# Two tiles of a chunked attention prepared a block earlier, and the second expert's rows turned on TensorE

## The chip, the cores and the metric

The kernel runs on one core of a Trainium2 chip. The metric is the device time of one execution in microseconds (us); below, "the median" is that of three runs. One further execution was profiled.

## The reference

Three layers follow each other: a gated linear attention, a gated two-matrix layer, and a layer of eight experts of which each token uses one.

```python
f = 1.0 / (1.0 + np.exp(-f_logit))                  # q, k, v, f_logit: 4 x 8 x 768 x 48
for t in range(S):                                  # per batch and head, state 48 x 48
    state = f[:, :, t, :, None] * state + np.einsum('bhd,bhe->bhde', k[:, :, t], v[:, :, t])
    y[:, :, t] = np.einsum('bhd,bhde->bhe', q[:, :, t], state)
x = y.transpose(0, 2, 1, 3).reshape(3072, 384)      # tokens x model
x = ((x @ w_a) * (x @ w_b)) @ w_out                 # 384 x 1536, 384 x 1536, 1536 x 384
logits = x @ w_gate; e_idx = argmax(logits, axis=1) # 8 experts
...
for e in range(8):                                  # w1: 384 x 1024, w2: 1024 x 384
    mask = e_idx == e
    ye = np.maximum(x[mask] @ w1[e], 0.0) @ w2[e]
    out[mask] = gate_w[mask, None] * eom[mask, e, None] * ye
```

## The kernel before, in words

Products in full precision are made of three passes on TensorE over a number split into a high and a low part (`xh`, `xl`; `wab` and `wo` hold both parts of the weights). Everything is unrolled; the program is one long list for each engine.

**Attention tiles.** The 768 positions of 4 batches are 24 tiles of 128 positions, `order[i] = (c, b)`: chunk by chunk, batch by batch. A tile goes through the steps of the list `steps` (L1038): `a_log` (step 0: sigmoid's logarithm on ScalarE, its halves `lh` and `ll`), `a_v` (1), `a_range` (2: sums of squares for a range test, and the loads of tile i+2), `a_cum` (3: a running sum on TensorE, L791 and L792, and two exponentials `eq`, `ek`), `a_q` (4), `a_z` and `a_vs` (5: the halves of q and k laid side by side in `z` by VectorE and GpSimd, then a DMA transpose of `z` into `zT` issued by SP at L835), `a_u` and `a_uh` (6: the state's decay and halves), `a_kv` (7), `a_score` (8: L919, L926 on TensorE, then `sm`, `Sh`, `Sl`), `a_av` (10), `a_turn` (12) and `a_x` (13: the tile turned, as `xh` and `xl`). Inputs and most tiles have two buffers.

**Blocks.** Two tiles make a block of 256 tokens, `j` from 0 to 11; a block needs 12 steps `f` of `m_ab` (L1063 to L1065), each followed by `asb` (ScalarE), `gf` (VectorE), `gh` (ScalarE), `gl` (GpSimd) and `m_out` (L1098 to L1100). `r_row`, `r_pick`, `r_rank` and `r_send` then choose each token's expert and scatter its place into `slots`.

**First phase.** The conversion of the weights, tiles 0 to 5 and blocks 0 and 1 are generators in the list `threads`, each with a start time. `in_time` (L508) runs a small model of the engines over them, picks in its order and chains each engine's instructions in that order. In the profile this phase ends at about 164 us.

**Later blocks.** For `j` from 2 to 11, step `f` runs `m_ab`, `m_out`, the routing of block j-1 and `attend(2j+2, f)`, which runs those steps of tiles 2j+2 to 2j+5 whose entry in the table `at` (L1262) is this `f`. So tiles 6 and 7 pass from step 1 (tile 7: from step 1 as well) to `a_x` while TensorE works on block 2, and tile 8 starts in its last step. Outside the first phase the framework orders each engine's list itself, by a simulation at build time in which program order is the priority; an instruction marked with `keep_in_program_order` (or `in_order`) stays behind all that was written before it on its engine. On the chip every engine then works through its list in order.

**Experts.** The first place (the fullest expert, e = 0) has 512 slots, worked on in two halves of 256, each with 8 steps `f`: `e_h` (L1465 to L1467: product, `h` by a Relu on ScalarE at L1479, the low part by VectorE at L1483) and, one step behind, `e_y` (the matmuls of L302 into `ps_out` and `ps_yk`). The rows come by gathers on GpSimd (`xs`, L1363); those of the first place are turned by TensorE in `to_columns` (L1453, then L1454 and L1455). The second place's rows (e = 1, four tiles, 480 slots) are turned as 16-bit halves: a copy on VectorE and a DMA transpose issued by SP in `e_turn` (L1425, L1430), and two copies on VectorE, one on ScalarE and a subtraction in `e_xT` (L1441 to L1446). Expert weights come in 8 pieces of 384 KB into `raw` (three buffers); `load_epiece` issues a load on SP and `split_expert` makes the halves on ScalarE (L1244) and VectorE (L1245), both kept in program order. Three pieces of the second place are loaded in the first place's first half and split in its steps 4 to 6; the other five are loaded and split in steps 0 to 4 of its second half:

```python
            if f == 2:
                e_gather(1)
                load_epiece(1, split=False)
            if f >= 4 and fetched:
                split_expert()
...
        elif half == 1:
            ahead(1, TURN1, XT1, f)
            load_epiece(1)
```

Of the kernel before, what the change touches and what calls it, by code (L numbers as in the profile page):

```python
# [305 lines left out]
def kernel(  # L306
# [413 lines left out]
    def a_log(i):  # L720
        yield op("ACT", 0.5, ("in_f", i))
        s = st[i]
        f = s["f"]
        nc.scalar.activation(out=f, in_=f, func=AF.Exp, scale=-1.0)
        yield op("ACT", 0.7, gives=("ln", i))
        nc.scalar.activation(out=f, in_=f, func=AF.Ln, scale=c_st, bias=c_st)
        yield op("DVE", 0.4, ("ln", i), ("cum", i - 1), gives=("lh", i))
        s["lh"] = tl("lh", [P, H, D], F16)
        nc.vector.tensor_copy(out=s["lh"], in_=f)
        yield op("DVE" if i < NFAST else "POOL", 0.6 if i < NFAST else 1.0, ("lh", i), gives=("ll", i))  # L730
        s["ll"] = tl("ll", [P, H, D], F16)
        fast(i).tensor_tensor(out=s["ll"], in0=f, in1=s["lh"], op=ALU.subtract)
# [85 lines left out]
    def a_z(i):  # L818
        yield op("DVE", 0.37, ("kx", i), ("T", i - 2), ("kv", i - 2), gives=("kh", i))
        s = st[i]  # L820
        z = s["z"] = z_n[i % NZ]
        qe, ek = [s[x].rearrange("p (a o) d -> p a o d", o=2) for x in ("qe", "ek")]
        kh, kl = z[:, :, 6:10:3, :D], z[:, :, 7:9, :D]
        nc.vector.tensor_copy(out=kh, in_=ek)
        yield op("DVE" if i < NFAST else "POOL", 0.58 if i < NFAST else 1.0, ("kh", i), gives=("kl", i))
        fast(i).tensor_tensor(out=kl, in0=ek, in1=kh, op=ALU.subtract)
        for o in range(2):
            yield op("DVE", 0.37, ("qe", i))
            q2 = qe[:, :, o, None, :].to_broadcast([P, HP, 2, D])
            nc.vector.tensor_copy(out=z[:, :, 2 * o : 2 * o + 2, :D], in_=q2)  # L830
        yield op("DVE", 0.58, gives=("ql", i))
        nc.vector.tensor_tensor(out=z[:, :, 4:6, :D], in0=qe, in1=z[:, :, 0:4:2, :D], op=ALU.subtract)
        yield op("SP", 3.1, ("ql", i), ("kl", i), ("scored", i - 2), *inter_of(i - 2), gives=("T", i), lands=0.6)
        s["T"] = tl("zT", [P, 5 * HP, P], F16, 2)
        nc.sync.dma_start_transpose(out=s["T"], in_=z.rearrange("p a c d -> p (a c d)"))  # L835

    def a_vs(i):
        yield op("DVE", 0.42, ("vv", i), ("kv", i - 1), gives=("vs", i))
        s = st[i]
        s["vs"] = tl("vs", [P, 2, H, D], F16)  # L840
        nc.vector.tensor_scalar(out=s["vs"], in0=s["vv"], scalar1=c_w, scalar2=None, op0=ALU.mult)

    def a_u(i):

        c, b = order[i]
        if c < NCH - 1:
            for o in range(2):
                yield op("SP", 0.45, ("gd", i), ("U", i - 2), gives=("g", i, o), lands=0.05)
                s = st[i]
                g = s["g"] = g_n[i % 2]  # L850
                nc.sync.dma_start(g[part(o)], s["gd"][:].rearrange("(a o) d -> d a o", o=2)[:, :, o])

    def a_uh(i):
        c, b = order[i]
        if c > 0:
            for o in range(2):
                yield op("ACT", 0.37, ("U", i - 2), *inter_of(i - 2), gives=("uh", i, o))
                s = st[i]
                u2, u3 = s["u2"], s["u3"] = U2[i % 2], U3[i % 2]
                hi, lo = u2[part(o), :, o], u2[part(1 - o), :, o]  # L860
                nc.scalar.activation(out=hi, in_=U[b][part(o)], func=AF.Copy)
                yield op("POOL", 0.6, ("uh", i, o))
                nc.gpsimd.tensor_tensor(out=lo, in0=U[b][part(o)], in1=hi, op=ALU.subtract)
                yield op("POOL", 0.4, gives=("u", i, o))
                nc.gpsimd.tensor_copy(out=u3[part(o), :, o], in_=hi)
# [146 lines left out]
    def a_x(i):  # L1012
# [23 lines left out]
        nc.vector.tensor_tensor(out=xl[:, :, ts], in0=x, in1=xh[:, :, ts].bitcast(F32), op=ALU.subtract)  # L1036

    steps = [  # L1038
        a_log, a_v, a_range, a_cum, a_q, lambda i: both(a_z(i), a_vs(i)), lambda i: both(a_u(i), a_uh(i)), a_kv,
        a_score, None, a_av, None, a_turn, a_x,  # L1040
    ]

    def both(x, y):
        yield from x
        yield from y
# [193 lines left out]
    def split_expert():  # L1239

        e, g, part, raw, tag, nk = fetched.pop(0)
        pair = ring_tile(tag)
        hi, lo = pair[:, :768], pair[:, 768:1536]
        in_order(tc, nc.scalar.activation)(out=hi, in_=raw, func=AF.Copy)  # L1244
        nc.vector.tensor_tensor(out=lo, in0=raw, in1=hi.bitcast(F32), op=ALU.subtract)  # L1245
        we[e, g, part] = (
            hi.rearrange("p (k f) -> p k f", k=nk),
            lo.rearrange("p (k f) -> p k f", k=nk),
        )
# [3 lines left out]
    def load_epiece(e, split=True):  # L1253
        if e < E and epieces[e]:
            load_expert(*epieces[e].pop(0))
            if split:
                split_expert()
# [8 lines left out]
    def route(j, f):  # L1266
# [5 lines left out]
        if f == 3:  # L1272
            r_rank(j)
            r_send(j)

    def attend(i0, f):

        for i, g in ((i0, f), (i0 + 2, f - NF)):
            for t in range(2):
                if i + t < NTILE:  # L1280
                    for n in range(14):
                        if at[t][n] == g and steps[n]:
                            run(steps[n](i + t) or ())

# [28 lines left out]
    for i in range(6):  # L1313
        for t, gen in (
            (0, a_log(i)), (3, a_v(i)), (2, a_cum(i)), (3, a_q(i)), (4, a_z(i)), (6, a_vs(i)), (4, a_u(i)), (4, a_uh(i)),
            (8, a_kv(i)), (9, a_score(i)), (12, a_av(i)), (14, a_x(i)),
        ):
            threads.append((T0[i] + t, gen))
    for n in range(len(batches)):
        t = C0 + CD * n  # L1320
        threads.append((t - 6, raw_load(n)))
        threads.append((t, (conv_o if batches[n][0] == "o" else conv_ab)(n)))
        if batches[n][0] == "o":
            threads.append((t - 9.4, gates(n)))
# [33 lines left out]
    def tiles_of(e):  # L1358

        return [(t, min(P, CAPS[e] - t)) for t in range(0, CAPS[e], P)]  # L1360
# [108 lines left out]
    def e_h(e, f, n=None):  # L1469

        us = slice(0, CAPS[e]) if e > 0 else slice(n * HALF, (n + 1) * HALF)
        size = us.stop - us.start
        ph = bank("ab")[:, :size]
        first_product(e, f, ph, us)

        h = ctl("h", [P, 2 * CAP], F32R, 4)
        t, m = tiles_of(e)[-1]
        cut = t if e > 0 and is_pair(m) else 0
        nc.scalar.activation(out=h[:, :size], in_=ph, func=AF.Relu)  # L1479
        for lo, hi in ((cut, size), (0, cut)):  # L1480
            if hi > lo:
                to = size + lo - cut if lo >= cut else 2 * size - cut + lo
                nc.vector.scalar_tensor_tensor(  # L1483
                    out=h[:, to : to + hi - lo],
                    in0=ph[:, lo:hi],
                    scalar=0.0,
                    in1=h[:, lo:hi].bitcast(F32),
                    op0=ALU.max,
                    op1=ALU.subtract,
                )  # L1490
        h_t[e, f, n] = (h, size, cut)
# [139 lines left out]
        nc.vector.tensor_reduce(out=bad, in_=tot, axis=AX, op=ALU.max)  # L1631
        nc.vector.tensor_copy(out=flag, in_=bad)

    TURN1, XT1 = [0, 0, 2, 2], [4, 5, 6, 7]
    TURN, XT = [2, 2, 3, 3], [4, 5, 6, 7]

    def ahead(e, turn, columns, f):

        for u in range(NU):
            if turn[u] == f:  # L1640
                e_turn(e, u)
            if columns[u] == f:
                e_xT(e, u)
# [50 lines left out]
    for n in range(1, 2 * NF2 + LAG):  # L1694
        half, f = divmod(n, NF2)
        if half < 2:
            e_h(0, f, half)
        if n >= LAG:
            done, fy = divmod(n - LAG, NF2)
            for u in range(2):  # L1700
                e_y(0, fy, 2 * done + u)
                if fy == NF2 - 1 and done == 0:
                    e_out(0, u)
        if half == 0:
            if f == 2:
                e_gather(1)
                load_epiece(1, split=False)
            if f >= 4 and fetched:
                split_expert()
            if f == 6:  # L1710
                for e in range(2, E):
                    find(e)
                    load_tab(e)
            if f == 7:
                for u in range(2):
                    to_columns(0, xs[0][:, 2 + u], slice((2 + u) * P, (3 + u) * P), idn)
        elif half == 1:
            ahead(1, TURN1, XT1, f)
            load_epiece(1)
    for e in range(1, E):  # L1720
        for f in range(NF2):
            e_h(e, f)
# [65 lines left out]
```

## Time and profile before

| what | value |
|---|---|
| median of 3 runs | 886.93 us (883.01 to 887.08) |
| the profiled execution, its own time | 891.19 us |
| its span, first to last instruction | 889.1 us |
| mean granted TensorE clock over the span | 0.973 of full speed |
| TensorE busy | 814.3 us, 92% of the span, 6733 matmuls |
| VectorE, ScalarE, GpSimd busy | 542.2, 450.7 and 300.3 us |

The profile is of one execution, and 4.3 us longer than the median; 2.1 us of it lie outside the span. Busy shares are means over stages that have different limits; places where TensorE stands idle are found by windows, and what it waits for by the waits and the timeline.

### The profile page before, as it was taken

How to read it: one execution, taken by the hardware profiler on the slowest of the kernel's cores; microseconds unless marked ns; L12 is line 12 of the kernel's file. 1: busy time of each engine (PE TensorE's matmuls, PEld its weight loads, DVE VectorE, ACT ScalarE, POOL GpSimd, SP SyncE). 2: the span in 40 equal slices, each digit the busy share in tenths (PEclk: the TensorE clock that was granted, in tenths of full speed). 3: DMA queues.
4: the chain of work that ended last, by engine and by line, in shares of the span. 5: the costliest groups of instructions: out<-in, count | busy, mean ns of one | idle time of the engine just before them, and what ended most of it. 6: DMA issues, size and time to landing. Idle time of an engine off the chain costs nothing.

```text
span 889.1 us, 17901 instructions
## 1 busy us (share of the span) xinstructions
PE 814.3 (92%) x6733; PEld 773.5 (87%) x6733; DVE 542.2 (61%) x1244; ACT 450.7 (51%) x1068; POOL 300.3 (34%) x383
## 2 busy tenths in 40 slices
PE   2599899969999999999999999999779999999993
PEld 1398799969999999999999899999779889899993
DVE  8899763636765656566666556436446665666730
ACT  5798765345655546555555453335224433544520
POOL 3013442535445444444444353220442123111111
PEclk9999799989999999999999999999889999999997
DMA  9997683481836262626270803005375585585610
GB/s 212 298 265 177 118 175 57 68 83 28 141 51 118 47 122 46 123 46 123 44 125 20 149 19 78 20 19 160 116 202 131 146 198 115 156 195 150 183 45 23
DMA packets 261578, 102.06 MB, mean 115 GB/s; under 512 B 229032, under 2 KB 252933, under 8 KB 261482
## 3 DMA queue, kind: packets, MB, share of 16 engines
q1 hardware_dynamic: 256362, 90.76, 47.6%
q0 software_dynamic: 4320, 10.03, 4.2%
q8 instruction: 55, 0.90, 0.5%
q14 instruction: 41, 0.34, 0.2%
q10 hardware_dynamic: 800, 0.02, 0.1%
HBM read 67.10 MB, written 10.49 MB: 87 GB/s over the span
## 4 chain that ended last, share of the span: by engine, by line
PE 61%; DMA 13%; issue 8%; DVE 8%; ACT 4%; SPq 3%; POOL 1%; another core or an unknown queue 1%; POOLq 0%; DVEq 0%; ACTq 0%
PE ps_ab L1063 10%; PE ps_ab L1064 9%; PE ps_ab L1065 9%; PE ps_out L1098 5%; PE ps_out L1099 5%; PE ps_out L1100 5%; DMA turned<-halves 4%; DMA in_f<-in_f_logit_dram 3%; PE ps_out L302 2%; PE ps_yk L302 2%; DMA raw<-in_moe_w_dram 2%; PE ps_ab L1465 2%; PE ps_ab L1466 2%; PE ps_ab L1467 2%; PE ps_yk L973 1%
## 5 line engine op out<-in xcount | busy, mean ns | idle before, releaser
L1063 PE MATMUL ps_ab<-xh,wab 128*128 128x256 f32 x864 | 247.9, 287 | 4.4 <-DVE gf L1071 3.5
L1064 PE MATMUL ps_ab<-xl,wab 128*128 128x256 f32 x864 | 244.1, 283 | 0.2
L1065 PE MATMUL ps_ab<-xh,wab 128*128 128x256 f32 x864 | 243.6, 282 | 0.0
L1080 POOL TENSOR_TENSOR gl<-gf,gh 128x256 fp32r<-128x256 f32 x135 | 105.8, 785 | 220.6 <-ACT gh L1077 214.9
L1063 PEld LDWEIGHTS ps_ab<-xh,wab 128*128 128x128 f32 x864 | 163.5, 189 | 9.8 <-DVE gf L1071 6.8
L1064 PEld LDWEIGHTS ps_ab<-xl,wab 128*128 128x128 f32 x864 | 163.5, 189 | 1.5 <-DVE xl L1036 0.9
L1065 PEld LDWEIGHTS ps_ab<-xh,wab 128*128 128x128 f32 x864 | 163.5, 189 | 0.8
L1071 DVE SCALAR_TENSOR_TENSOR gf<-ps_ab,asb 128x256 f32<-128x256 f32 x144 | 60.2, 419 | 76.7 <-ACT asb L1068 73.7
L1098 PE MATMUL ps_out<-wo,gh 128*128 128x400 f32 x288 | 103.3, 359 | 2.9 <-ACT ex L1146 2.5
L1099 PE MATMUL ps_out<-wo,gh 128*128 128x400 f32 x288 | 100.5, 349 | 0.0
L1077 ACT ACTIVATE gh<-gf 128x256 fp32r<-128x256 f32 x144 | 59.9, 416 | 79.4 <-DVE gf L1071 76.4
L1100 PE MATMUL ps_out<-wo,gl 128*128 128x400 f32 x288 | 98.5, 351 | 0.0
L1068 ACT ACTIVATE asb<-ps_ab 128x256 f32<-128x256 f32 x144 | 54.4, 378 | 68.1 <-PE ps_ab L1065 67.7
L1539 POOL DMA_INDIRECT out_dram<-ys,tab x29 | 30.0, 1033 | 166.7 <-ACT ys L1534 160.3
L1465 PE MATMUL ps_ab<-xsh,wab 128*128 128x256 f32 (+5 forms) x216 | 74.1, 344 | 4.5 <-DVE h L1483 4.5
L1466 PE MATMUL ps_ab<-xsl,wab 128*128 128x256 f32 (+5 forms) x216 | 73.7, 341 | 0.1
L1467 PE MATMUL ps_ab<-xsh,wab 128*128 128x256 f32 (+5 forms) x216 | 73.5, 340 | 0.0
L1479 ACT ACTIVATE h<-ps_ab 128x256 fp32r<-128x256 f32 (+5 forms) x72 | 34.7, 483 | 76.1 <-PE ps_ab L1467 51.2
L1483 DVE SCALAR_TENSOR_TENSOR h<-ps_ab,h 128x64 fp32r<-128x64 f32 (+5 forms) x96 | 41.2, 451 | 39.8 <-ACT h L1479 39.5
L1245 DVE TENSOR_TENSOR wab<-raw,wab 128x768 fp32r<-128x768 f32 x48 | 45.8, 956 | 31.9 <-ACT wab L302 26.9
L1098 PEld LDWEIGHTS ps_out<-wo,gh 128*128 128x128 f32 x288 | 55.0, 191 | 4.1 <-ACT ex L1146 3.1
L302 ACT ACTIVATE wab<-raw 128x768 fp32r<-128x768 f32 x48 | 40.3, 841 | 31.5 <-DMA raw<-in_moe_w_dram 31.1
(241 smaller groups left out, 1700.8 us busy)
## 6 DMA issues: line engine op xcount, KB each, us to landing
raw<-in_moe_w_dram SPq DMA_DIRECT2D x64, 384.0 KB
in_f<-in_f_logit_dram SPq DMA_DIRECT2D x24, 192.0 KB
in_q<-in_q_dram SPq DMA_DIRECT2D x24, 192.0 KB
in_k<-in_k_dram SPq DMA_DIRECT2D x24, 192.0 KB
in_v<-in_v_dram SPq DMA_DIRECT2D x24, 192.0 KB
wab<-in_moe_w_a_dram SPq DMA_DIRECT2D x6, 768.0 KB
wab<-in_moe_w_b_dram SPq DMA_DIRECT2D x6, 768.0 KB
wo<-in_moe_w_out_dram SPq DMA_DIRECT2D x6, 768.0 KB
```

The costliest lines, as they stand in the source:

```text
L302: return lambda *a, **k: tc.keep_in_program_order(op(*a, **k))
L1063: nc.tensor.matmul(pab[:, a], wh[:, kk, o : o + P], xh[:, kk], start=(kk == 0), stop=False)
L1064: nc.tensor.matmul(pab[:, a], wh[:, kk, o : o + P], xl[:, kk], start=False, stop=False)
L1065: nc.tensor.matmul(pab[:, a], wl[:, kk, o : o + P], xh[:, kk], start=False, stop=(kk == KD - 1))
L1071: nc.vector.scalar_tensor_tensor(out=gf, in0=pab[:, 1], scalar=2.0**-WS, in1=asb, op0=ALU.mult, op1=ALU.mult)
L1080: (nc.vector if last else nc.gpsimd).tensor_tensor(out=gl, in0=gf, in1=gh.bitcast(F32), op=ALU.subtract)
L1098: nc.tensor.matmul(o, gh[:, ts], wh[:, u], start=(f == 0), stop=False)
L1099: nc.tensor.matmul(o, gh[:, ts], wl[:, u], start=False, stop=False)
L1100: nc.tensor.matmul(o, gl[:, ts], wh[:, u], start=False, stop=(f == NF - 1))
L1465: nc.tensor.matmul(ph, wh[:, kk, o : o + P], sh[:, kk, us], start=(kk == 0), stop=False)
L1466: nc.tensor.matmul(ph, wh[:, kk, o : o + P], sl[:, kk, us], start=False, stop=False)
L1467: nc.tensor.matmul(ph, wl[:, kk, o : o + P], sh[:, kk, us], start=False, stop=(kk == KD - 1))
```

## The change

Two parts of the program are rearranged.

First, `a_log`, `a_v`, `a_cum`, `a_q`, `a_z`, `a_u` and `a_uh` of tiles 6 and 7 become threads of the first phase, with start times 110 and 118; `attend` leaves out these steps (the tuple `begun`) for tiles below 8, and step 5 runs `a_vs` alone for them. `a_range`, `a_vs`, `a_score` and what follows stay where they were.

Second, for the first place (e = 0) every Relu of `e_h` is kept in program order on ScalarE. No piece of the second place's weights is split in the first half any more: each step of the second half issues one load (as long as there are pieces) and makes one split, so the eight splits fall on its eight steps. The second place's rows are turned by `to_columns` on TensorE in steps 4 to 7 of the second half, one tile a step; its `e_turn` and `e_xT` go away. Experts 2 to 7 are as before.

```diff
     steps = [
-        a_log, a_v, a_range, a_cum, a_q, lambda i: both(a_z(i), a_vs(i)), lambda i: both(a_u(i), a_uh(i)), a_kv,
+        a_log, a_v, a_range, a_cum, a_q, lambda i: a_vs(i) if i < NPE + 2 else both(a_z(i), a_vs(i)), lambda i: both(a_u(i), a_uh(i)), a_kv,
         a_score, None, a_av, None, a_turn, a_x,
     ]
...
+    begun = (0, 1, 3, 4, 6)
+
     def attend(i0, f):
 
         for i, g in ((i0, f), (i0 + 2, f - NF)):
             for t in range(2):
                 if i + t < NTILE:
                     for n in range(14):
+                        if i + t < NPE + 2 and n in begun:
+                            continue
                         if at[t][n] == g and steps[n]:
                             run(steps[n](i + t) or ())
...
+    for i in range(NPE, NPE + 2):
+        for gen in (a_log(i), a_v(i), a_cum(i), a_q(i), a_z(i), a_u(i), a_uh(i)):
+            threads.append((110 + 8 * (i - NPE), gen))
...
-        nc.scalar.activation(out=h[:, :size], in_=ph, func=AF.Relu)
+        ins = nc.scalar.activation(out=h[:, :size], in_=ph, func=AF.Relu)
+        if e == 0:
+            tc.keep_in_program_order(ins)
...
-    TURN1, XT1 = [0, 0, 2, 2], [4, 5, 6, 7]
...
             if f == 2:
                 e_gather(1)
                 load_epiece(1, split=False)
-            if f >= 4 and fetched:
-                split_expert()
...
         elif half == 1:
-            ahead(1, TURN1, XT1, f)
-            load_epiece(1)
+            if f == 0:
+                xsT[1] = (ctl("xsh", [P, KD, CAP], F32R, 2), ctl("xsl", [P, KD, CAP], F32R, 2))
+            if f >= 4:
+                t, m = tiles_of(1)[f - 4]
+                to_columns(1, xs[1][:m, f - 4], slice(t, t + m), idn[:m, :m])
+            load_epiece(1, split=False)
+            split_expert()
```

## Rows read from the trace of the kernel before

**Rows 1.** Windows of core 0: time, busy time of each engine, granted clock, DMA share, GB/s.
```profile
119.00:164.00 45.00, 45.00 (x427) 43.62 (x426) 17.43 (x41) 25.62 (x74) 13.39 (x21) 1.00 0.44 86
164.00:204.00 40.00, 31.98 (x321) 29.86 (x321) 24.61 (x61) 18.05 (x51) 18.84 (x22) 0.91 0.79 88
204.00:564.00 360.00, 356.69 (x3494) 341.51 (x3493) 227.76 (x559) 190.47 (x513) 164.32 (x218) 1.00 0.44 78
...
634.00:645.00 11.00, 6.14 (x27) 5.54 (x27) 4.44 (x7) 4.24 (x8) 7.46 (x7) 0.69 0.68 198
645.00:671.00 26.00, 20.97 (x124) 20.03 (x123) 13.88 (x30) 8.95 (x19) 10.28 (x10) 0.87 0.66 179
```

**Rows 2.** Timeline of TensorE, 176 to 200 us; in brackets the wait before.
```profile
179.92 0.40 PE L919 MATMUL ps_at<-zT 128*128 128x128 f16 x4 [1.40 <-DMA zT<-z]
...
186.43 0.59 PE L919 MATMUL ps_at<-zT 128*128 128x128 f16 x4 [4.99 <-DVE dj L1193]
...
189.07 0.41 PE L1063 MATMUL ps_ab<-xh,wab 128*128 128x256 f32 x1
...
189.70 0.28 PE L1063 MATMUL ps_ab<-xh,wab 128*128 128x256 f32 x1
```

**Rows 3.** Timelines of SP, ScalarE and VectorE, 164 to 202 us.
```profile
169.94 3.02 SPq L835 DMA_TRANSPOSE zT<-z  x1
173.02 0.57 SPq L302 DMA_DIRECT2D in_f<-in_f_logit_dram  x1
...
177.94 9.38 SPq L835 DMA_TRANSPOSE zT<-z  x1
...
184.56 0.52 ACT L724 ACTIVATE in_f<-in_f 128x384 f32<-128x384 f32 x1 [5.98 <-DMA in_f<-in_f_logit_dram]
...
185.86 0.36 DVE L729 CAST lh<-in_f 128x384 f16<-128x384 f32 x1 [7.73 <-ACT in_f L726]
```

**Rows 4.** Timeline of TensorE, 630 to 702 us.
```profile
637.18 1.01 PE L302 MATMUL ps_out<-wab,h 128*128 128x384 f32 x2 [3.23 <-ACT wab L302]
639.87 0.90 PE L1453 MATMUL ps_at<-idn,xs 128*128 128x128 f32 x3 [1.69 <-DMA xs<-x2d,tab]
...
644.07 0.49 PE L1453 MATMUL ps_at<-idn,xs 128*128 128x128 f32 x3
...
645.14 0.51 PE L1465 MATMUL ps_ab<-xsh,wab 128*128 128x256 f32 x2
...
658.47 2.29 PE L302 MATMUL ps_yk<-wab,h 128*128 128x384 f32 x6 [4.80 <-ACT h L1479]
...
668.52 0.28 PE L1465 MATMUL ps_ab<-xsh,wab 128*128 128x256 f32 x1
...
670.64 0.37 PE L1465 MATMUL ps_ab<-xsh,wab 128*128 128x480 f32 x1
```

**Rows 5.** Timelines of ScalarE, SP and GpSimd, 612 to 700 us.
```profile
636.01 0.84 ACT L302 ACTIVATE wab<-raw 128x768 fp32r<-128x768 f32 x1 [5.82 <-DMA raw<-in_moe_w_dram]
...
658.04 0.38 ACT L1479 ACTIVATE h<-ps_ab 128x256 fp32r<-128x256 f32 x1 [6.90 <-remote]
...
632.83 1.02 SPq L302 DMA_DIRECT2D raw<-in_moe_w_dram  x2
...
636.05 1.01 POOL L1363 DMA_INDIRECT xs<-x2d,tab  x1 [0.31 <-issue]
```

**Rows 6.** Waits: ScalarE 204 to 600 us, TensorE 200 to 600 and 60 to 160.
```profile
ACT in_f L724 <- DMA in_f<-in_f_logit_dram: 26.8, 9, 4.7
...
PE ps_out L1098 <- ACT ex L1146: 1.8, 1, 1.8
...
PE ps_at L791 <- POOL ll L732: 0.7, 1, 0.7
```

**Rows 7.** The chain that ended last, 620 to 700 us: start, length, what.
```profile
634.70 4.76 DMA xs<-x2d,tab
...
687.26 6.79 DMA raw<-in_moe_w_dram
```

## What the change was predicted to do

> **What bounds the kernel now.** I read the windows first. TensorE is busy 814.3 of 889.1 us by the page, and in the long middle it is the bound without a doubt: 3.3 us idle in 360 us, about 0.4 in 40 us [rows 1]. So a change can win only where TensorE is not fed, and I looked for those places. Two lie where this change works. Place A, 164 to 204 us, is block 2: 8.0 us idle. Place B, 634 to 671 us, is the middle and second half of the first expert's place: 4.9 and 5.0 us idle. In both the granted clock is under 1, so part of the work ran at 1.2 instead of 2.4 GHz [rows 1]. The other idle stretches (the start, and the last expert's end) are not touched.
>
> Then the timelines, to see what TensorE waited for. In A it is 1.4 us for the DMA transpose of tile 6 and 5.0 us for VectorE [rows 2]. VectorE was late because a cast for tile 8 (L729) stood in its list behind the logarithm of ScalarE, which waited 5.98 us for the load of `in_f` [rows 3]. That load was issued at 173.02, right behind the transpose of tile 6 that held SP for 3.02 us, and landed at 184.5, 11.5 us later; the transpose of tile 7 then held SP for another 9.38 us [rows 3]. So the reader is to see that an input load for the next tiles, late among two transposes, stops two engines that work through fixed lists. After it the products ran at 1.2 GHz (one 0.41 us long) up to 189.7, where they are 0.28 us again [rows 2].
>
> In B the first stop is ScalarE standing 5.82 us in the split of a weight piece while finished products wait for their Relu behind it; TensorE loses 3.23 us, and then waits 1.69 us more for the gathered rows of the second half [rows 4, 5]. The second stop is 4.80 us before 658.47. The Relu that ends it began at 658.04 after 6.90 us of idleness for which the profile names no releaser ("remote") [rows 4, 5]; I know only that the second expert's four DMA transposes, which the change removes, run there.
>
> **The change part by part, place A.** Running sum, exponentials, `z`, its transpose and the state's halves of tiles 6 and 7 move into block 1, 119 to 164 us. Is there room? TensorE is full there (45.00 of 45), but VectorE has 27.6, ScalarE 19.4 and GpSimd 31.6 us free. All that these three did in 164 to 204 (24.6, 18.1, 18.8), block 2's own work included, would fit, and the moved part is less than that [rows 1]. SP's two transposes go past the stores and loads of block 1, at 3 us each as the first one shows [rows 3]. So I cost the moved work at nothing on these engines. If that cover failed, the wait would fall on TensorE, whose fixed list holds the two running sums in between products. The nearest row is a running sum of an earlier tile that waited 0.7 us for its operand [rows 6]: 0 to 1.4 us for two; I take 0.7.
>
> What is won: 8.0 us idle, and the 3.3 us from 186.43 to 189.70 at the lower clock, which cost 1.6: 9.6 us. What is late next is tiles 8 and 9, whose loads and logarithms keep their places; they no longer queue behind two transposes. In the middle stretch ScalarE still waits nine times for `in_f`, 26.8 us together, and TensorE hardly notices [rows 1, 6]. The rest of idleness is then between 0.4 us (a mean 40 us of the middle) and everything but the 1.4 us wait for the transpose. I leave 2.0, near the middle's end, since the jam of SP is what differs from the middle. A: 9.6 - 2.0 - 0.7 = 6.9 us; ends 9.2 and 0.
>
> Here the trace speaks against a rule. A transpose held SP 3.02 and 9.38 us where the load of `in_f` took 0.57, and TensorE saw tile 6's transpose landed at 179.92, 10.0 us after its issue [rows 2, 3]. The Trainium skill, "Advanced Engine Details and Errata", section "X-Bar Transpose (TRN2)", says that "TRN2 transpose DMAs are as fast as regular DMAs". By that rule moving them frees little, the late load stays late, and the third rival below is what happens; by the rows the sum stands.
>
> **Place B.** The three splits leave the first half, so no Relu stands behind a load there. From 633.95 (where the 3.23 us wait begins) TensorE has left two products of first-half steps and what follows them, two pairs; a pair takes 2.12 us (668.52 to 670.64) [rows 4]: done at 638.2. Then it must wait for the gather: the first landed at 639.46, the second was issued at 636.05, and with the same 4.76 us lands at 640.8 [rows 5, 7]. From the transposes to the next product took 1.07 us (644.07 to 645.14) [rows 4]; with 0.4 for the start, as between 639.46 and 639.87, the second half starts at 642.3 instead of 645.14.
>
> From there to the second expert's first product it took 25.5 us (645.14 to 670.64). The work in it now is 7.5 pairs, 15.9 us, since the first half's last `e_y` is already done, and the new cost, four tiles turned on TensorE at 0.49 us each [rows 4], 2.0 us. The second expert starts at 642.3 + 17.9 = 660.2, which is 10.4 us earlier. The copies taken off VectorE and the four transposes off SP are not on the path and count as nothing. From this I take off three things.
>
> The clock: after the long wait the work from 639.87 to 645.14 ran under a window mean of 0.69, 5.3 us at 1.2 GHz at the most, which costs 2.6 [rows 1, 4]; the wait that is left is shorter, so 0 to 2.6, and I take 1.3.
>
> The weights: pieces 4 to 8 each need one of three buffers, which comes free only after a split in this half. One turn of a buffer is the load, 0.4 us of issue, 0.84 of cast [rows 5] and about 1 for the subtraction; a load took 3.2 us (632.83 to 636.01) at best and 6.8 at worst [rows 5, 7]. At 3.2 a turn is 5.4 us, at 6.8 it is 9.0, against three steps of 2.12, 6.4 us. Two turns: 0 to 5.3 us late. Behind a late split stand the next Relu on ScalarE and so TensorE. I take 1.5, as the stretch has fewer transfers than the one with 6.8.
>
> The Relu's fixed place behind the routing's exponentials and row copies at about 623 us: 0 to 1 us, I take 0.3, since other products are ready.
>
> B: 10.4 - 1.3 - 1.5 - 0.3 = 7.3 us; ends 10.4 and 1.5. [...]
>
> **Sum.** 6.9 + 7.3 = 14.2 us: the profiled execution would go from 891.2 to 877.0. It lies 4.3 us above the median of the runs, so I take 14.2 off 886.9: 872.7 us.
>
> **The rivals.** (1) The weight loop sets the pace: loads at 6.8 us take all 5.3. B is 10.4 - 1.3 - 5.3 - 0.3 = 3.5, the total 876.5. For it: one turn at 3.2 is already close to three steps; against: loads of 384 KB were mostly quicker than 6.8.
> (2) The nameless wait stays, having nothing to do with the transposes: 4.8 us, and 1.2 by which the six matmuls behind it were slow (2.29 us for 1.06) [rows 4]. B is 1.3, total 878.7.
> (3) `in_f` of tile 8 stays late: ScalarE's list lets tile 8's logarithm in before its load is there. A is 1.4 - 0.7 = 0.7, total 878.9. For it: the nine waits of the middle; against: those cost TensorE nearly nothing.
> (4) The change does not do what it says: waits (2) and (3) both stay and merely move. A 0.7, B 1.3: 884.9.
> (5) Slower: with tiles 6 and 7 early, the framework orders every later block anew, and each of the nine blocks 3 to 11 gets one wait of TensorE. The longest single wait in the middle is now 1.8 us [rows 6], the longest in A 5.0. From (14.2 + 4.4) / 9 = 2.1 us a block on, the kernel is slower by over 0.5%; at 2.5 us, half of A's, it takes 886.9 - 14.2 + 22.5 = 895.2. Against it: the table `at` is unchanged and the middle has 3.3 us idle in all.
>
> **How the numbers follow.** Chances: forecast 0.42, (1) 0.13, (2) 0.12, (3) 0.12, (4) 0.13, (5) 0.08. The best end is 886.9 - 9.2 - 10.4 = 867.3; the range reaches from 867 to 884, takes in (1) to (3) and stops before (4) and (5), which leaves out about 2 in 10. A measurement of this kernel can tell about 0.5%, 4.4 us, from no change. Faster by more: forecast and (1) to (3), 0.79; within: (4), 0.13; slower: (5), 0.08.
>
> **What would show it.** Right for A: both `zT` issues of tiles 6 and 7 before 164 us, no wait of L919, idleness of 164 to 204 at 2 us or less, block 1 still full. Right for B: no split before 640 us, TensorE idle only before the first-place transposes, no "remote" Relu, `e_turn` absent for the second place, its first product about 10 us earlier after A's gain is taken off. Wrong: ScalarE waiting for `raw` in every step of the second half, L724 waiting 6 us again, or waits spread over blocks 3 to 11.

## The result and the profile after

The changed kernel takes 879.67 us (median of 8 runs, 876.51 to 881.33) against 887.09 for the kernel before (8 runs), a ratio of 0.9916 with a 95% interval of 0.9887 to 0.9946. That is 7.4 us less, half of the 14.2 that I forecast; 879.67 lies inside the range of 867 to 884, seven above the 872.7. Measured once more beside other kernels (e8 below) the ratio was 0.9895 (0.9853 to 0.9937). The profiled execution took 880.73 us, its span 878.8.

The windows of the kernel after, with the columns of [rows 1]:

```profile
119.00:164.00 45.00, 44.17 (x439) 41.85 (x434) 27.62 (x66) 29.12 (x88) 19.65 (x26) 1.00 0.61 121
164.00:204.00 40.00, 38.16 (x405) 36.21 (x404) 16.86 (x51) 18.19 (x50) 15.10 (x21) 1.00 0.44 56
204.00:564.00 360.00, 355.54 (x3447) 340.77 (x3446) 227.05 (x556) 189.56 (x509) 162.81 (x217) 0.99 0.44 79
...
645.00:671.00 26.00, 24.97 (x158) 23.62 (x157) 17.23 (x28) 13.09 (x24) 10.39 (x10) 1.00 0.58 183
```

In place A TensorE now stands idle 1.8 us (8.0 before) and its granted clock is 1.00, the 2.4 GHz level. VectorE did 10.2 us more in 119 to 164 and the DMA share rose there from 0.44 to 0.61, while it fell from 0.79 to 0.44 in 164 to 204: the moved work is where it was meant to be. Block 1 is no longer quite full: TensorE is idle for 0.8 us from 119 to 164. The waits of TensorE from 164 to 262 us (us in total, times, longest), where the 5.0 and 1.4 us before L919 of [rows 2] stood:

```profile
PE ps_ab L1063 <- DVE gf L1071: 0.9, 1, 0.9
PE ps_yk L973 <- DVE Sl L958: 0.5, 1, 0.5
PE ps_ab L1065 <- issue: 0.4, 1, 0.4
```

SP of the kernel after, 139 to 176 us, answering to [rows 3]: both transposes are issued before 155 us, and the loads of `in_f` of tiles 8 and 9 follow 16 and 20 us later.

```profile
140.86 3.08 SPq L835 DMA_TRANSPOSE zT<-z  x1
...
151.04 3.01 SPq L835 DMA_TRANSPOSE zT<-z  x1
...
170.45 0.69 SPq L302 DMA_DIRECT2D in_f<-in_f_logit_dram  x1
...
174.16 0.91 SPq L302 DMA_DIRECT2D in_f<-in_f_logit_dram  x1
```

Place B of the kernel after, TensorE (answers to [rows 4]) and ScalarE (answers to [rows 5]):

```profile
638.49 0.55 PE L1461 MATMUL ps_at<-idn,xs 128*128 128x128 f32 x3 [3.50 <-DMA xs<-x2d,tab]
638.79 0.59 PE L302 MATMUL ps_out<-wab,h 128*128 128x384 f32 x2
...
639.62 1.63 PE L302 MATMUL ps_out<-wab,h 128*128 128x384 f32 x4
...
641.54 0.78 PE L1473 MATMUL ps_ab<-xsh,wab 128*128 128x256 f32 x2
...
659.61 0.62 PE L302 MATMUL ps_yk<-wab,h 128*128 128x384 f32 x2 [0.59 <-ACT h L1487]
660.67 0.97 PE L302 MATMUL ps_yk<-wab,h 128*128 128x384 f32 x4 [0.44 <-DVE h L1493]
661.47 0.38 PE L1473 MATMUL ps_ab<-xsh,wab 128*128 128x480 f32 x1
```

```profile
635.03 0.38 ACT L1487 ACTIVATE h<-ps_ab 128x256 fp32r<-128x256 f32 x1 [1.73 <-PE ps_ab L1475]
639.07 0.49 ACT L1462 ACTIVATE xsh<-ps_at 128x384 fp32r<-128x384 f32 x1 [3.66 <-PE ps_at L1461]
...
644.54 0.84 ACT L302 ACTIVATE wab<-raw 128x768 fp32r<-128x768 f32 x1
...
654.56 0.85 ACT L302 ACTIVATE wo<-raw 128x768 fp32r<-128x768 f32 x1 [1.34 <-DMA raw<-in_moe_w_dram]
...
658.44 0.84 ACT L302 ACTIVATE wo<-raw 128x768 fp32r<-128x768 f32 x1 [2.77 <-DMA raw<-in_moe_w_dram]
```

No split of the second place's weights comes before 644.54, no Relu stands behind one in the first half, TensorE's one real stop in the first half is the 3.50 us for the gathered rows, and the wait of 4.80 us of [rows 4] is gone. The four matmuls at 639.62 took 0.41 us each where 0.24 is usual (0.97 for 4 at 660.67): the lower clock after the stop, as forecast. In the second half ScalarE waits 4.3 us for weight pieces and TensorE 1.0.

So each step looks as predicted. To see what each is worth I cut every profile of this study at the same instructions of ScalarE: the first `asb` of block 1 and of block 4 (place A with its surroundings), the last `asb` of block 11, and the seventeenth Relu, the second expert's first (place B). All in us:

| kernel | ratio to before, 95% interval | block 1 to 4 | block 11 to second expert |
|---|---|---|---|
| before / again (e9) | | 143.4 / 148.9 | 55.3 / 50.8 |
| e1, first part alone / again (e10) | 0.9918 (0.9886 to 0.9949) | 137.0 / 137.6 | 49.4 / 51.4 |
| e2, second part alone | 0.9979 (0.9937 to 1.0021) | 145.4 | 46.2 |
| e3, splits and pin alone | 0.9968 (0.9929 to 1.0007) | 149.1 | 49.4 |
| e4, turn alone | 0.9981 (0.9947 to 1.0015) | 148.5 | 48.3 |
| after / again (e8) | 0.9916 / 0.9895 | 138.2 / 138.1 | 47.4 / 46.2 |
| e5, tile 6 only | 0.9974 (0.9951 to 0.9996) | 144.1 | 46.4 |
| e6, later start times | 0.9954 (0.9928 to 0.9980) | 144.0 | 46.8 |
| e7, splits in the gap | 0.9912 (0.9880 to 0.9944) | 138.3 | 49.3 |
| e11, no pin | 0.9892 (0.9836 to 0.9948) | 137.3 | 48.0 |
| e12, five pieces ahead | 0.9919 (0.9894 to 0.9944) | 137.5 | 49.2 |

### The profile page after: what moved, and what is told of

It is laid out like the page before. It is cut to its first block, busy times and chain, and to the rows that moved or that the text cites. A ratio compares the mean times of both kernels' runs of the same rounds, so it can differ in the third digit from the quotient of the medians.

```text
span 878.8 us, 17919 instructions
## 1 busy us (share of the span) xinstructions
PE 813.8 (93%) x6745; PEld 774.6 (88%) x6745; DVE 537.4 (61%) x1232; ACT 451.9 (51%) x1068; POOL 298.6 (34%) x383
## 4 chain that ended last, share of the span: by engine, by line
PE 61%; DMA 12%; issue 10%; DVE 6%; ACT 4%; SPq 3%; POOL 1%; POOLq 0%; DVEq 0%; ACTq 0%
PE ps_ab L1063 9%; PE ps_ab L1065 9%; PE ps_ab L1064 9%; PE ps_out L1098 5%; PE ps_out L1099 5%; PE ps_out L1100 5%; PE ps_out L302 3%; DMA turned<-halves 3%; DMA raw<-in_moe_w_dram 2%; PE ps_yk L302 2%; PE ps_ab L1473 2%; PE ps_ab L1474 2%; DMA in_f<-in_f_logit_dram 2%; PE ps_ab L1475 2%; SPq L302 2%
## 5 line engine op out<-in xcount | busy, mean ns | idle before, releaser
L1098 PEld LDWEIGHTS ps_out<-wo,gh 128*128 128x128 f32 x288 | 55.3, 192 | 3.0 <-ACT ex L1146 2.3
L1099 PEld LDWEIGHTS ps_out<-wo,gh 128*128 128x128 f32 x288 | 55.5, 193 | 0.0
```

The costliest lines, as they stand in the source:

```text
L1098: nc.tensor.matmul(o, gh[:, ts], wh[:, u], start=(f == 0), stop=False)
L1099: nc.tensor.matmul(o, gh[:, ts], wl[:, u], start=False, stop=False)
```

## The experiments

The theory at the start was that both parts do what their named waits say, place A is partly paid back in block 1, and the nameless wait of place B (the 4.80 us of [rows 4]) belongs to the DMA transposes. The rivals were that one part does it all, and that the nameless wait has another cause.

**e1, the first part alone.** The whole change with the experts' edits undone:

```diff
-        ins = nc.scalar.activation(out=h[:, :size], in_=ph, func=AF.Relu)
-        if e == 0:
-            tc.keep_in_program_order(ins)
+        nc.scalar.activation(out=h[:, :size], in_=ph, func=AF.Relu)
...
+            if f >= 4 and fetched:
+                split_expert()
...
+            ahead(1, TURN1, XT1, f)
+            load_epiece(1)
```

> The first part of the change alone (tiles 6 and 7 begun in the first phase), the experts as before. Theory: the two parts add up. In the traces of before and after, block 3 began 4.6 us earlier and block 10 only 0.4 us earlier; if both come from this part, the time is 1 to 4.5 us under the kernel before (ratio 0.995 to 0.999), block 1's seventh step is again some 7 us late, and place B has both its waits (5.8 us of ScalarE before the split, and the Relu without a releaser). Rival: the loss in blocks 9 and 10 belongs to the second part, and this part alone keeps the whole 4.6 us or more (0.992 to 0.995).

Measured: 0.9918, as much as the whole change. From step 5 of block 3 on (steps are counted from 0), the lists of all five engines are those of the kernel before, instruction by instruction; yet the Relu without a releaser did not appear in place B, which took 49.4 us instead of 55.3. The time is the rival's, if not for its reason: up to the experts the lists of e1 and of the whole change are the same, so the loss in blocks 9 and 10 does not belong to the second part; from block 4 to the end of block 11 the same lists took 354.3 us here, 355.7 in e10, 356.0 in the trace after and 353.8 in e8. The theory on the nameless wait is in doubt.

**e2, the second part alone.** The kernel before with only the experts' edits.

```diff
-            if f >= 4 and fetched:
-                split_expert()
...
-            ahead(1, TURN1, XT1, f)
-            load_epiece(1)
+            if f >= 4:
+                t, m = tiles_of(1)[f - 4]
+                to_columns(1, xs[1][:m, f - 4], slice(t, t + m), idn[:m, :m])
+            load_epiece(1, split=False)
+            split_expert()
```

> The second part alone (splits in the second half, Relu pinned, rows turned on TensorE), the attention as before. Theory: the second expert's first product comes about 8 us earlier and the later experts add up to 3 us more, so 8 to 11 us under the kernel before (ratio 0.988 to 0.991), nearly all of what the whole change gave. Rival: the gain needs the first part too, because the routing and the gathers reach place B earlier with it: then 4 to 5 us (0.995).

Measured: 0.9979, not to be told from no change. Theory and rival both miss: 46.2 us in place B is as little as any profile has (e8 has it too), so the edit works, but it is not worth 8 us.

**e3 and e4, the halves of the second part.** In e3 the rows are still turned by DMA, in e4 the splits stay and the Relu is not pinned.

```diff
 # e3, against e2
-            if f >= 4:
-                t, m = tiles_of(1)[f - 4]
-                to_columns(1, xs[1][:m, f - 4], slice(t, t + m), idn[:m, :m])
+            ahead(1, TURN1, XT1, f)
 # e4, against e2
...
+            if f >= 4 and fetched:
+                split_expert()
...
-            load_epiece(1, split=False)
-            split_expert()
+            load_epiece(1)
```

> The second part without its last piece: the splits moved to the second half and the Relu pinned, but the second expert's rows turned by DMA transposes as before. Theory: the wait of 4.80 us before 658.47 belongs to the four DMA transposes, so it stays, and only the first stop (3.2 us) goes: 3 to 4 us under the kernel before (0.995 to 0.997). Rival: the wait came from the order of splits and loads and goes with them: as much as the whole second part, 8 us or more (0.991 or less).

> Of the second part only the turning on TensorE; the splits stay in the first half's steps 4 to 6 and the Relu is not pinned. Theory: the second stop (4.8 us) goes and the first (ScalarE standing 5.8 us in a split, TensorE 3.2 us) stays: 4 to 6 us under the kernel before (0.993 to 0.995). Rival: with the DMA transposes gone the split order alone costs as much as before and the wait only moves: 0 to 2 us (0.998 to 1.0).

Measured: 0.9968 and 0.9981, neither surely below 1. By these times e3 fits its theory and e4 its rival, but the intervals do not tell them apart. In e3 the transposes are all there and no Relu waits without a releaser: the theory that they bring that wait each time falls. In e4 ScalarE again stands 6.0 us in a split and TensorE 3.5 us behind it, and the second half takes 18.9 us.

**e5 and e6, less of the first part.** In e5 only tile 6 is begun early; in e6 the moved threads have later start times.

```diff
 # e5
-    for i in range(NPE, NPE + 2):
+    for i in range(NPE, NPE + 1):
...
-                        if i + t < NPE + 2 and n in begun:
+                        if i + t < NPE + 1 and n in begun:
 # e6
-            threads.append((110 + 8 * (i - NPE), gen))
+            threads.append((150 + 8 * (i - NPE), gen))
```

> The whole change, but only tile 6 is begun in the first phase; tile 7 stays in block 2. Theory: block 2 lost its time because the load of tile 8's in_f stood on SP behind the transpose of tile 6, so tile 6 alone keeps most of the gain: the wait of L919 for VectorE (5.0 us before) is at 1 us or less, block 1 to block 4 takes 137 to 140 us (146.6 in the mean of four profiles without the first part, 137.6 with it), and the time is within 2 us of the whole change. Rival: any transpose in block 2 jams SP, tile 7's takes the place of tile 6's, and 4 us or more of the gain are lost (ratio 0.995 or more).

> The whole change with start times 150 and 158 for the moved threads in place of 110 and 118, so that the planner lets more of block 1's own products go first. Theory: with the first part, block 1 took 46.1 us from its first step to block 2's first step, against 43.9 without it; some of these 2.2 us come back (1 to 2 us faster than the whole change) as long as both transposes are still issued before 168 us. Rival: the moved work only arrives later, tile 7's transpose falls into block 2, and the wait for in_f or zT is there again: 2 to 5 us slower than the whole change.

Measured: 0.9974 and 0.9954; both rivals hold, and two thirds of place A's gain are lost. The longest wait of TensorE from 160 to 265 us in e5, and SP and ScalarE there:

```profile
PE ps_ab L1063 <- DVE gf L1071: 7.6, 1, 7.6
```

```profile
169.36 0.69 SPq L302 DMA_DIRECT2D in_f<-in_f_logit_dram  x1
...
178.38 2.94 SPq L835 DMA_TRANSPOSE zT<-z  x1
...
182.07 0.63 SPq L302 DMA_DIRECT2D in_f<-in_f_logit_dram  x1
```

```profile
173.43 0.53 ACT L724 ACTIVATE in_f<-in_f 128x384 f32<-128x384 f32 x1 [0.54 <-DMA in_f<-in_f_logit_dram]
...
192.60 0.52 ACT L724 ACTIVATE in_f<-in_f 128x384 f32<-128x384 f32 x1 [11.06 <-DMA in_f<-in_f_logit_dram]
```

The reader sees that tile 8's load, ahead of the one transpose that is left, was used 4.1 us after its issue (169.36 to 173.43); tile 9's, behind it, 10.5 us after (182.07 to 192.60), and ScalarE with its whole list stood still for 11.06. In e6 both transposes come early in block 2 and are over on SP before the load is issued:

```profile
165.51 3.49 SPq L835 DMA_TRANSPOSE zT<-z  x1
...
170.27 3.02 SPq L835 DMA_TRANSPOSE zT<-z  x1
...
174.95 1.39 SPq L302 DMA_DIRECT2D in_f<-in_f_logit_dram  x1
```

```profile
186.43 0.52 ACT L724 ACTIVATE in_f<-in_f 128x384 f32<-128x384 f32 x1 [8.97 <-DMA in_f<-in_f_logit_dram]
```

The load still needed 11.5 us. The trace marks when each transfer lands: tile 7's transpose landed at 181.8 in e6 and at 188.6 in e5, 11.5 and 10.2 us after its issue, when SP had long gone on, and the load behind it landed 4.6 and 4.0 us after that. Alone, in block 1 of the trace after, a transpose landed 5 us after its issue. So it isn't SP's order alone, which I had named: the transpose's data is still on its way after SP is free.

But a load can be as late without a transpose. These are the DMA views from 160 to 200 us, one column for each us, of e6 and then of the kernel after: the busy share of the DMA engines in tenths (9 is 90% or more) and what they moved.

```profile
DMA  0000067999259973986899998995956899200000
GB/s 0 2 0 1 0 224 218 137 223 233 32 106 213 218 137 40 55 16 17 19 24 44 59 112 136 99 42 28 106 90 104 179 195 178 48 0 0 0 0 0
```

```profile
DMA  0000000001989999954996766710000000000270
GB/s 0 0 25 0 0 0 0 0 0 63 310 167 221 214 190 189 85 21 30 84 49 15 49 63 90 128 26 0 0 0 0 0 16 0 0 0 0 54 143 0
```

In e6 the engines are 6 to 9 tenths busy from 176 to 183 us and move only 16 to 59 GB/s; in the kernel after they are 4 to 9 tenths busy from 176 to 185 and move 15 to 90, and there both transposes had landed by 156. In all seven profiles with both tiles begun early, tile 9's load was used 10.2 to 11.5 us after its issue; in the five with neither, tile 8's was used 11.5 to 12.4 us after. So the transposes do not make the load slow, or not alone; why the engines move so little is open. What the first part changes in every profile is which load is the slow one and when it is issued. Tile 8's goes out 2.3 us behind block 2's first `asb` where it was 9.1, and is used 3.6 to 4.1 us later; the slow one is tile 9's, issued 5.5 to 6.1 us behind that `asb`, where in e5 it is 16.4. There SP's order did count: the load stands behind a transpose that waits for its own tile. With a transpose in block 2 TensorE's longest wait there is 4.9 to 7.6 us; with none it is 1.7 us at most.

**e7, splits where ScalarE is idle.**

```diff
             if f == 7:
+                for _ in range(3):
+                    split_expert()
+                for _ in range(3):
+                    load_epiece(1, split=False)
...
-            load_epiece(1, split=False)
-            split_expert()
+            if fetched:
+                split_expert()
+            load_epiece(1, split=False)
```

> The whole change, but three splits (and the loads of the next three pieces) are written into the first half's last step, behind its Relu, where ScalarE stood idle from 635.5 to 644.5 us waiting for the gathered rows; the other five splits are in steps 0 to 4 of the second half. Theory: the second half took 20.1 us because the weight loop runs late (ScalarE waited 4.3 us for pieces in its steps 5 to 7); with the buffers free 8 us earlier these waits go, the second half takes 18 to 19 us and the time is 1 to 2 us under the whole change. Rival: TensorE had other work there and the weight loop cost it nothing: same time, the second half again about 20 us.

Measured: 0.9912, the same as the whole change, but by neither theory: the second half grew to 22.0 us. The splits did come at 633.4 to 637.8, but the loads behind them stood on SP behind the tables of the other experts (`tab`) until 642.10, as in this timeline of SP:

```profile
638.72 2.60 SPq L1602 DMA_DIRECT2D tab<-slots  x3
641.51 0.33 SPq L1605 DMA_DIRECT2D tab<-slots  x1
642.10 13.04 SPq L302 DMA_DIRECT2D raw<-in_moe_w_dram  x7
```

ScalarE then waited 3.74 us for the first of these pieces, in front of a Relu. A miss, of the edit more than of the idea.

**e8, the whole change again.** No edit.

> The whole change once more, beside the others on one chip and with a second profile. Theory: the first part gives nearly all of it, so the ratio is 0.990 to 0.992, the same as the first part alone (0.9918) or up to 3 us under it; block 1 to block 4 takes 137 to 139 us and no Relu without a releaser stands in place B. Rival: the second part has an effect of its own as large as forecast (7 us), which the first run missed: 0.984 to 0.986.

Measured: 0.9895, 138.1 us in place A and 46.2 in place B, as the theory has it.

**e9 and e10, second profiles of the kernel before and of the first part alone.** No edit.

> The kernel before, profiled once more. Theory: the wait without a releaser (ScalarE 6.90 us, TensorE 4.80 us) was an event of that one execution, since the first part alone, whose lists from block 4 on are those of the kernel before, did not show it; it is absent here, from the last step of block 11 to the second expert's first product is 49 to 50 us (55.3 in the first profile, 49.4 with the first part alone), and block 1 to block 4 is again 143 to 149 us. Rival: it belongs to the program and comes back with 4 us or more.

> The first part alone, profiled once more. Theory: block 1 to block 4 is 137 to 139 us, as in its first profile and in the two of the whole change; the stretch from the last step of block 11 to the second expert's first product is 49 to 50 us and shows no Relu without a releaser. Rival: the wait without a releaser is as likely here as in the kernel before, and one in a few executions has it: then it may stand here, with 55 us.

Measured: 892.09 and 883.20 us in one execution each. ScalarE of the kernel before, second profile, at the place of the 6.90 us "remote" of [rows 5]:

```profile
652.68 0.39 ACT L1479 ACTIVATE h<-ps_ab 128x256 fp32r<-128x256 f32 x1 [0.89 <-PE ps_ab L1467]
654.80 0.39 ACT L1479 ACTIVATE h<-ps_ab 128x256 fp32r<-128x256 f32 x1 [1.73 <-PE ps_ab L1467]
659.27 0.52 ACT L1445 ACTIVATE xsh<-xst 128x384 fp32r<-128x384 f32 x1 [4.09 <-DVE xst L1441]
659.71 0.37 ACT L1479 ACTIVATE h<-ps_ab 128x256 fp32r<-128x256 f32 x1
```

Every Relu that waited has its releaser. What is left is a stop that the trace explains: a copy of the DMA-turned rows (L1445) stands before a Relu for 4.09 us, and costs TensorE 2.3. The wait without a releaser stood in one of the four profiles that have these lists (before, e9, e1, e10), the one that I had read; how often it comes in runs that were not profiled is not known. e10 was as expected in place A and 1.4 us over in place B. The waits of TensorE from 160 to 265 us in e9:

```profile
PE ps_at L919 <- DVE dj L1193: 5.1, 1, 5.1
PE ps_ab L1063 <- DVE gf L1071: 3.0, 1, 3.0
PE ps_at L919 <- DMA zT<-z: 1.7, 1, 1.7
```

The 3.0 us are new beside [rows 2]; e2, e3 and e4 have 1.4 to 1.8 of them. So for place A my profile was the mildest of five.

**e11, without the pin.**

```diff
-        ins = nc.scalar.activation(out=h[:, :size], in_=ph, func=AF.Relu)
-        if e == 0:
-            tc.keep_in_program_order(ins)
+        nc.scalar.activation(out=h[:, :size], in_=ph, func=AF.Relu)
```

> The whole change without keeping the first place's Relu in program order. Theory: the pin costs 0.3 us, between 0 and 1; without it the time is the same within the measurement and the first Relus come up to 1 us earlier. Rival: without the pin the framework puts splits before a Relu again, and ScalarE stands in one for 2 us or more.

Measured: 0.9892, the same within the measurement, and no Relu stood in a split. The second Relu came 1.4 us earlier (5.5 us behind block 11's last step, 7.0 with the pin), but the second half's first came 1.1 later (28.4 against 27.3 us). The pin costs nothing.

**e12, five pieces ahead.**

```diff
+            if f == 4:
+                two = htl("turned", [P, NU, 2 * KD, P], U16).rearrange("p u k t -> p (u k t)").bitcast(F32)
+                spare += [two[:, : 2 * DM], two[:, 2 * DM :]]
+            if f in (4, 5):
+                load_epiece(1, split=False)
...
-            load_epiece(1, split=False)
             split_expert()
+            load_epiece(1, split=False)
```

> The whole change with two more weight pieces loaded ahead: pieces 4 and 5 go in the first half's steps 4 and 5 into two buffers cut from the room of the tile that held the transposed halves, which the second place no longer uses; in the second half a split goes before the load of its step. Theory: the weight loop is what makes the second half 20 us instead of 17.9 (ScalarE waits 4 to 7 us for pieces there); with five pieces ahead these waits go to 2 us or less, the second half takes 18 to 19 us, and the time is 0 to 2 us under the whole change. Rival: TensorE's own work sets the second half (its products, four tiles turned, and late rows) and it stays at 19 to 20 us.

Measured: 0.9919, no gain. The second half took 18.6 us (20.1 and 18.9 in the two profiles of the whole change), so the weight loop costs it 0.3 to 1.5. But the first half grew from 27.3 to 30.6: the two loads, issued at 630.79, run beside the gather, and from 608 to 690 us TensorE waited 5.9 us for its rows, 3.5 in both profiles of the whole change. That the loads slow the gather is argued from this one profile:

```profile
PE ps_at L1462 <- DMA xs<-x2d,tab: 5.9, 2, 4.5
```

No kernel of these is surely faster than the change itself.

## Why the prediction was right or wrong

**Place A: right in kind, with its reason too narrow.** Block 1 to block 4 takes 147.0 us in the mean of five profiles without the first part (143.4 to 149.1) and 137.7 in seven with it (137.0 to 138.3): 9.3 us, where I had 6.9 with an upper end of 9.2. Two terms were off and partly cancel. The cost in block 1 was 2.4 us, not 0.7 (46.1 us from block 1's to block 2's first step, 43.7 without); 1.3 of it are the two running sums themselves, four matmuls of 0.33 to 0.34 us, which block 2 then saves. Blocks 2 and 3 gained 11.8, not 7.6 (103.3 to 91.5); 3.1 of the difference is that the execution I read was the mildest, with 100.2 there. Against that one alone place A gains 5.7. The late `in_f` was the right wait, but I blamed the jam on SP's order alone. e5 shows that one transpose in block 2 is enough, though SP is free before the load; and the kernel after shows a load as slow with no transpose near, at a place where it costs TensorE 0.9 us.

The rule that I set aside holds here per byte. The Trainium skill, "Advanced Engine Details and Errata", section "X-Bar Transpose (TRN2)", has transpose DMAs as fast as regular ones. I compared per instruction, 3.02 against 0.57 us. But a `zT` holds 128 x 20 x 128 numbers of 16 bits, 640 KB, and a load 192 KB. In the trace after the second transpose runs alone behind 151.04: it keeps the DMA engines busy for 20.3% of 151 to 168 us, 3.5 us, and moves 205 to 219 GB/s; the loads at 171 to 176 us move 167 to 221. So the measurement agrees with the rule. What hurts is the transpose's size and its place in SP's list. I concluded from the rule that the late load would stay late: tile 8's did not, tile 9's is.

**Place B: the trace after fits, the gain does not.** Put at the time of the trace before (block 11 ended 1.25 us earlier), the second half starts at 642.8 (forecast 642.3) and the second expert at 662.7 (forecast 670.64 - 7.3 = 663.3). What failed is the other end, "it took 25.5 us (645.14 to 670.64)": 4.80 us of that, and the slow matmuls behind it, are not in the other three profiles with these lists. From block 11's end to the second expert, the kernel before needs 50.5 us without that wait (e1, e9, e10: 49.4 to 51.4), the whole second part 46.6 (after, e8, e2, e5, e6: 46.2 to 47.4): 3.9 us, not 7.3. About 2.1 of them are the splits gone from the first half (27.3 for 29.4; forecast 2.8), 1.8 the second half. There I had counted the copies of the DMA-turned rows at nothing; in e1 and e9 TensorE stands 1.9 and 2.3 us once behind them. The weight loop cost 0.3 to 1.5 (e12; I took 1.5), the pin nothing (e11; 0.3). The lower clock was paid: 0.7 us on those four matmuls alone, besides what else ran until it rose (1.3 taken).

**The rivals.** (1) is refuted by e12: with five pieces ahead the second half is 0.3 to 1.5 us shorter, not 5.3. (2) is what decided, upside down: the nameless wait does not come with the transposes (e1, e3, e9 and e10 have them without it), yet it did not stay; in three of the four profiles with these lists it was not there to be won. (3) fell in its price: ScalarE still waits 4.70 us for `in_f` of tile 9 in the trace after, but at a place in its list where TensorE loses 0.9. (4) did not happen: neither wait is in the trace after. (5) did not happen: from block 4 to the end of block 11 it is 353.4 us without and 354.9 with the first part, ranges that overlap.

**Sum.** -9.3 in place A, -3.9 in place B, +1.5 in the middle, +1.8 behind the last Relu (below): 9.9 us, against 7.4 by the medians and 9.3 by the ratio of e8 (7.8 by its medians). The stretch from the second expert's first Relu to the last one is left out: it took 197.1 and 198.4 us in the two profiles of the kernel before and 194.0 and 195.1 in those of the whole change, but 194.0 and 194.3 in e1 and e10, whose lists there are the kernel before's, so it can be given to neither part. That the time fell inside the range owes something to luck: place A gave 2.4 us more than forecast and place B 3.4 less, and 3.3 went in two stretches that the forecast had at nothing. 879.67 is next to where rivals (2) and (3) put it (878.7 and 878.9), and neither happened as described. That the second part adds to the first is seen in the profiles, not in the times: 0.9918 without it, 0.9916, 0.9895 and 0.9892 with it or nearly all of it.

## What to carry to other kernels

A wait for which the trace names no releaser should not be priced until a second execution shows it; and a stop that the trace does explain can be larger or smaller in the next execution, so cut several profiles at the same instructions before a gain is counted in single microseconds. Where an input load stands behind a DMA transpose in one engine's list, move the transpose out of the stage altogether: with one of two away, or both a little earlier, place A still took 144.1 and 144.0 us, where it is 147.0 with both in block 2 and 137.7 with neither. And look at which instruction waits for the load: one as slow cost TensorE 5 us in the kernel before and 0.9 in the kernel after.

## What the runs showed of the hardware that I had not expected

A load of 192 KB issued 3.7 or 4.7 us after a DMA transpose of 640 KB was used 10.5 and 11.5 us after its issue, though the transpose had left SP 0.8 and 1.7 us before; one issued ahead of it took 4.1. The transpose itself landed 10.2 and 11.5 us after its issue there, and after 5 us where it ran alone. In the trace after, the second of two sets of loads also took 11.2 us (174.16 to 185.37) with no transpose near, so the transpose is not the only thing that slows them. In these stretches the DMA engines were busy and moved 15 to 90 GB/s, where they reach 220 a few us before; what slows them is open.

The same lists of instructions differed between executions by 5.5 us in place A (143.4 and 148.9, before and e9) and by 4.6 in place B (55.3 and 50.8); with the first part, place A differed by 1.3 in seven profiles. What held ScalarE for 6.90 us in the first profile is open.

From the last Relu to the end of the span took 18.8 to 19.2 us in the five profiles in which no tile was begun early, and 20.6 to 21.2 in the nine others, with the same lists at the end: 1.8 us, behind the last scatter. Why is open.
